# A circular 7x7 convolution of a 224x224 image on one core: reordered first loads, two weight jobs moved ahead of the first products, and a different place for one plane operation

## The chip, the cores and the metric

The kernel runs on one core of a Trainium2 chip. The metric is the device time of one execution in microseconds; lower is better. The core has a matrix engine (PE in the profile, with its weight loads shown as PEld), a vector engine (DVE), an activation engine (ACT), a general engine (POOL) and a queue engine (SP) that here mostly issues transfers between HBM and on-chip memory. The matrix engine writes into PSUM, an on-chip memory of eight banks; DVE and ACT move its results out ("evacuate" them), and each bank can be written again only once its evacuation is done.

## The reference

The input x is one image of 224 x 224 pixels with 96 channels, and w is a 7 x 7 kernel of 96 x 96 weights, both in bf16. The reference multiplies their two-dimensional Fourier transforms and transforms back, so the result is a circular convolution: the rows and columns before the first are the last ones.

```python
wp = jnp.pad(w, ((0, H - K), (0, W - K), (0, 0), (0, 0)))
Xf = rfft2(x.astype(f32), axes=(1, 2))
Wf = rfft2(wp.astype(f32), axes=(0, 1))
Yf = jnp.einsum('bhwi,hwio->bhwo', Xf, Wf)
y = irfft2(Yf, s=(H, W), axes=(1, 2)).astype(bf16)
```

## The kernel before

The kernel transforms along the image's rows only (h), in eight blocks of 28 rows with an overlap of six, and does the taps along w as shifted products with a minimal-filter scheme. A block's transform has 17 frequencies (`NS`), numbered s; frequency 0 and 16 are real (`REAL`) and cost fewer operations, the others are complex and use three products instead of four. The width is cut into seven tiles of 32 columns (`NT`), numbered t.

One tile goes through these steps. Its pixels are loaded by two transfers for each half of the blocks (`load_x`: 112 rows and 6 rows of 3,072 values each). The PE multiplies them with a Fourier matrix `Fm`, which a dozen small operations build at the start, and DVE or ACT evacuate the result into `xf` (functions `a_bank` and `f_jobs`). For groups of up to three frequencies (`JGB`), function `jit` makes three DVE operations, the "plane operations": the first and second write sums and differences of `xf` into the tile `J`, and the third adds parts of `J` into its planes 5 and 6. For every frequency, `b_round` then issues the products of `J` and `xf` with the transformed weights `WF` into two banks, an ACT copy with a factor (tile `tt_`), two DVE combinations `u` and `v`, and a sum of `u` and `v` into `yf`, which POOL does, or DVE in those rounds of tiles 2 to 6 that have plane operations (`ydve`). `yf` is written to a scratch array in HBM, read back as `tt` in another layout, multiplied with the inverse matrix `Gm`, evacuated into `yo` and stored (`c_jobs`).

The transformed weights are made by `prep_jobs(gi)` for six groups of frequencies (`PGRP`). The weights are loaded first, in five column pieces of two transfers each (`wdma`). A job of `prep_jobs` is four small PE products of the raw weights `wq` with a matrix `Em`, and one evacuation into `WF`; every group has 12 such jobs, and all but the first then have one DVE subtraction `WF<-WF` for each complex frequency. `evac` chooses DVE or ACT for an evacuation by running sums of costs, `load["v"]` and `load["a"]`.

All instructions of an engine run in the order in which the program issues them (`_Ordered`). At the start SP issues the wrap-around columns (`xh_bufs`, six columns left of the first tile, two transfers for each half), then the first half of the first tile's pixels, then the weights, then the second half. Every transfer of SP takes the next of eight completion counters in turn, so the ninth transfer is issued only when the first has landed, the tenth when the second has, and so on. The PE runs 17 products of zeros (`warm`), the wrap-around products, those of the first pixel half, 22 more products of zeros, the 48 products of weight group 0, those of the second half, and then the rounds. Tiles 0 and 1 run together, four rounds apart (`LAG`): from round 4 on, a round of tile 0 and one of tile 1 alternate. Within a round, `mid` and `end` run waiting jobs from lists with due times (`add`, `pace`): weight jobs of the next group and pixel jobs of tiles 1 and 2. For tiles 0 and 1 the plane operations of a group are put behind a round's `v` (`bursts`): two of the three in one round, and the third in the next round (`rest`), for both tiles alike. In a round with two plane operations the POOL sum waits for the second (line 580).

The steps that the change touches are lines 178 to 181 (first loads), 577 to 580 (what the POOL sum waits for), 707 to 711 (zero products and the jobs before the first products), 744 and 745 (due times of the weight jobs) and 795 to 797 (how many plane operations go into a round).

Of the kernel before, what the change touches and what calls it, by code (L numbers as in the profile page):

```python
# [56 lines left out]
def kernel(  # L57
# [117 lines left out]
    def load_x(t, jg):  # L175
        return load_rows(xbuf(t, jg), jg, t * 2 * TW, 2 * TW)

    wsrc = w.rearrange("kh kw i o -> (kh kw) (i o)")
    for jg in range(2):
        load_rows(xh_bufs[jg], jg, W - PAD, PAD)  # L180
    load_x(0, 0)
    wcut = [WC * c // NWC // 128 * 128 for c in range(NWC)] + [WC]
    wdma = []
    for c0, c1 in zip(wcut, wcut[1:]):
# [281 lines left out]
    def jit(t, g):  # L466
        s0, s1 = JGB[g]
        n = s1 - s0
        xf = xf_tiles[t][0:C]
        xv = xf.rearrange("c p r s w j -> c p r s (w j)")  # L470
        b = jcount[0] % 3 if t < 2 else (jcount[0] - 2 * len(JGB)) % 2
        jcount[0] += 1
        Jb = J_bufs[b][0:C].rearrange("c (k s q) -> c k s q", k=7, s=3)
        for s in range(s0, s1):
            jbuf[(t, s)] = Jb[:, :, s - s0]

        def sub(o, a, b, op, cost):
            def f():
                load["v"] += 170 + cost / 1.92
                return VE.tensor_tensor(out=o, in0=a, in1=b, op=op)  # L480
            return f
        x0, x1 = xv[:, 0, :, s0:s1], xv[:, 1, :, s0:s1]
        c0, c1 = max(s0, REAL[0] + 1), min(s1, REAL[1])
        i0, i1 = c0 - s0, c1 - s0
        pd, rd, sd, qd = x1.ap
        dpl = bass.AP(x1.tensor, x1.offset - NJ, [pd, [NJ, 2], rd, sd, qd])
        return [
            sub(Jb[:, 0:4, 0:n].rearrange("c (k r) s q -> c k r s q", r=2), dpl,
                x0.unsqueeze(1).to_broadcast([C, 2, 2, n, PP]), ALU.subtract, 4 * PP * n),
            sub(Jb[:, 4, i0:i1], xv[:, 0, 0, c0:c1], xv[:, 0, 1, c0:c1], ALU.add, PP * (c1 - c0)),  # L490
            sub(Jb[:, 5:7, i0:i1], Jb[:, 0:4:2, i0:i1], Jb[:, 1:4:2, i0:i1], ALU.add, 2 * PP * (c1 - c0)),
        ]
# [3 lines left out]
    def b_round(t, s, mid, end, ydve=False, planes=()):  # L496
# [26 lines left out]
        if s in REAL:  # L523
            for part in range(2):
                conv(b0, part * C, 0, part)
            SE.copy(out=tt_[:, 0:2 * C], in_=b0[:, 0:2 * C])
            mid()
            for mi, m in enumerate((2, 1)):
                for part in range(2):
                    conv(b1, (mi * 2 + part) * C, m, part)  # L530
            VE.tensor_tensor(out=yv.rearrange("p r m o -> p m r o"),
                             in0=tt_[:, 0:2 * C].rearrange("p (r o) -> p r o", o=C).unsqueeze(1).to_broadcast([128, 2, 2, C]),
                             in1=b1[:, 0:4 * C].rearrange("p (m r o) -> p m r o", m=2, r=2), op=ALU.add)
            load["a"] += 110 + 0.9 * 192
            load["v"] += 540
            for f in planes:
                f()
            end()
        else:
            v = tv_pool.tile([128, 2, 2, C], F32, name="v")  # L540
            if merge:
                conv(b0, 2 * C, 0, 0, both=True)
                conv(b0, 2 * C, 2, 0, add=True)
                conv(b0, 3 * C, 1, 0, add=True)
                conv(b0, 0, 0, 1)
                conv(b0, C, 0, 2)
                SE.mul(out=tt_[:], in_=b0[:, 0:4 * C], mul=-0.5)
                u, pr = tt_[:, 2 * C:4 * C].rearrange("p (m o) -> p m o", m=2), tt_[:, 0:2 * C]
            else:
                for part in range(3):  # L550
                    conv(b0, part * C, 0, part)
                conv(b0, 3 * C, 2, 0)
                conv(b0, 4 * C, 1, 0)
                u = tv_pool.tile([128, 2, C], F32, name="u")
                SE.mul(out=tt_[:, 0:3 * C], in_=b0[:, 0:3 * C], mul=-0.5)
                pr = tt_[:, C:3 * C]
            if puts:
                puts.pop(0)()
            if not merge:
                VE.scalar_tensor_tensor(out=u[:], in0=b0[:, 3 * C:5 * C].rearrange("p (m o) -> p m o", m=2), scalar=-0.5,  # L560
                                        in1=tt_[:, 0:C].unsqueeze(1).to_broadcast([128, 2, C]), op0=ALU.mult, op1=ALU.add)
            mid()
            for mi, m in enumerate((2, 1)):
                for pi, part in enumerate((1, 2)):
                    conv(b1, (mi * 2 + pi) * C, m, part)
            VE.scalar_tensor_tensor(out=v.rearrange("p m r o -> p m (r o)"),
                                    in0=pr.unsqueeze(1).to_broadcast([128, 2, 2 * C]), scalar=-2.0,
                                    in1=b1[:, 0:4 * C].rearrange("p (m q) -> p m q", m=2), op0=ALU.mult, op1=ALU.add)
            def ysum(eng):
                return eng.tensor_tensor(out=yv.rearrange("p r m o -> p m r o"), in0=v[:],  # L570
                                         in1=u.unsqueeze(2).to_broadcast([128, 2, 2, C]), op=ALU.add)
            if ydve:
                ysum(VE)
            last = None
            for f in planes:
                last = f()
            if not ydve:
                y = ysum(GE)
                if len(planes) > 1:
                    tc.add_manual_dep(y.ins, last.ins.name, SYNC, reason="sum after planes")  # L580
            load["a"] += 490 if merge else 410
            load["v"] += (560 if ydve else 250 if t < 2 else 0) + (560 if merge else 900)
            end()
# [120 lines left out]
    for p in range(3):  # L704
        for f in fj[p][0]:
            f()
    for n in (11, 11):
        warm(n)
    for f in prep_jobs(0):
        f()  # L710
    last = [f() for f in fj[0][1]]
    for jg in range(2):
        for d in load_x(1, jg):
            tc.add_manual_dep(d.ins, last[0].ins.name, SYNC, reason="second tile's pixels later")
# [26 lines left out]
    def add(a, b, jobs):  # L741
        qs.append([a, b, jobs, len(jobs)])

    for gi in range(1, len(PGRP)):
        add(2 * PGRP[gi - 1][0], 2 * PGRP[gi - 1][1] - (2 if gi == 1 else 1), prep_jobs(gi))
    for t in range(2):
        scr_tiles[t] = dr_pool.tile([TW, NJ, NS, 4 * C], BF16, name="scr")
    bursts = {}
# [9 lines left out]
    for r in range(NS + LAG):  # L758
        if r == 0:
            add(1, 5, fj[1][1])  # L760
            add(5, 9, fj[2][1])
        for p in range(3):
            if r == (1, 3, 5)[p]:
                new_xf(1, SH2[p], SH2[p + 1])
                fj = f_jobs(1, p)
                if p == 2:
                    for jg in range(2):
                        fj[jg][-1] = then_load(fj[jg][-1], 2, jg)
                add(2 * r + 1, 2 * r + (5, 5, 4)[p], fj[0] + fj[1])
        for p in range(3):  # L770
            if r == SH2[p + 1] + 1 - (p == 2):
                new_xf(2, SH2[p], SH2[p + 1])
                fj = f_jobs(2, p)
                if p == 2:
                    for jg in range(2):
                        fj[jg][-1] = then_load(fj[jg][-1], 3, jg)
                add(2 * r, 2 * r + (8, 7, 5)[p], fj[0] + fj[1])
        if r == PGRP[-2][1] + 1:
            assert not any(q[2] for q in qs[:len(PGRP) - 1])
            wtmp_cm.__exit__(None, None, None)  # L780
            t_pool = ctx.enter_context(tc.tile_pool(name="tt", bufs=NTT, side="right"))
            t2_pool = ctx.enter_context(tc.tile_pool(name="tt2", bufs=1, side="right"))
            yo_pool = ctx.enter_context(tc.tile_pool(name="yo", bufs=2, side="right"))
            g_pool = ctx.enter_context(tc.tile_pool(name="gp", bufs=1, side="right"))
            GA = g_pool.tile([KA, 4 * B], BF16, name="GA")
            GB = g_pool.tile([128, 2, 4 * B], BF16, name="GB")
            GE.memset(GA[:], 0.0)
            GE.memset(GB[:], 0.0)
        if r == NS + 3:
            queue_c(0)  # L790
        for t in range(2):
            s = r - LAG * t
            if not 0 <= s < NS:
                continue
            now = bursts.pop((r, t), ())
            now = jit(*now) if now else []
            now, rest = rest + now[:2], now[2:]
            both = LAG <= r < NS
            b_round(t, s, fills(qs, 2 * r + (t if both else 0)), fills(qs, 2 * r + (t if both else 1)), False, now)
    assert not rest and not bursts and nburst == 2 * len(JGB)  # L800
# [111 lines left out]
```

## Time and profile before

| what | value |
|---|---|
| median of three runs | 270.54 us (270.21 to 270.58) |
| the profiled execution's own time | 270.74 us |
| its span, first to last instruction | 269.0 us |
| granted PE clock, mean | 0.997 |
| PE busy | 257.9 us, 96% of the span, 5144 products |
| PE weight loads busy | 237.1 us, 88% |
| DVE busy | 214.3 us, 80% |
| ACT busy | 195.5 us, 73% |
| POOL busy | 99.4 us, 37% |
| HBM traffic | 24.65 MB read, 21.33 MB written |

The busy times of the engines overlap. PE's share is near the whole span, so the time is set by the PE's work and by the places where it waits; those are read from the chain of work that ended last and from the list of waits. The times in the views count from the first instruction of the core, and the whole execution takes 1.74 us more than the span.

### The profile page before, as it was taken

The page shows a single profiled execution, that of the slowest core. Times are in us where ns is not written, and L with a number is a line of the kernel's source. Part 1 is how long each engine was busy: PE and PEld are TensorE (multiplying, and loading weights), DVE is VectorE, ACT ScalarE, POOL GpSimd, SP SyncE. Part 2 cuts the span into 40 slices and gives each one's busy share as a digit, 9 for nine tenths or more (in the row PEclk, how much of TensorE's full clock was granted, in tenths as well). Part 3 has the DMA queues.
Part 4 walks back from the last instruction along what each step waited for, and adds up shares of the span by engine and source line. Part 5 has one row for each costly group of instructions (what it writes and reads, how often), then busy time and mean ns, then how long its engine had stood idle before and what let it go on. Part 6 is the DMA issues. An engine that isn't in the chain of part 4 may idle for free.

```text
span 269.0 us, 12171 instructions
## 1 busy us (share of the span) xinstructions
PE 257.9 (96%) x5144; PEld 237.1 (88%) x5144; DVE 214.3 (80%) x457; ACT 195.5 (73%) x483; POOL 99.4 (37%) x156
## 2 busy tenths in 40 slices
PE   8899999999999999999999999999998999899993
PEld 3679999999998999999999998989997989779862
DVE  5649998889899788778787888777887889778724
ACT  5549988587974578988988789886986864467113
POOL 7782315363647435322322222234132242522100
PEclk9999999999999999999999999999999999999998
DMA  6948011811111597987976486989658834888866
GB/s 171 230 129 217 6 46 46 243 47 67 46 46 50 163 276 135 294 249 206 289 207 198 133 246 192 250 223 332 224 151 152 255 98 154 198 231 212 223 118 205
DMA packets 47014, 46.78 MB, mean 174 GB/s; under 512 B 35286, under 2 KB 37986, under 8 KB 46960
## 3 DMA queue, kind: packets, MB, share of 16 engines
q1 hardware_dynamic: 44672, 43.94, 59.2%
q10 hardware_dynamic: 2288, 2.06, 2.8%
q8 instruction: 40, 0.66, 1.1%
q14 instruction: 14, 0.11, 0.1%
HBM read 24.65 MB, written 21.33 MB: 171 GB/s over the span
## 4 chain that ended last, share of the span: by engine, by line
PE 64%; DMA 12%; DVE 11%; ACT 7%; issue 3%; SPq 2%; DVEq 0%; ACTq 0%
PE pb L89 64%; DMA tt<-scr 5%; DMA wq<-in_w_dram 5%; DVE J L89 4%; ACT WF L89 3%; ACT xf L89 2%; DVE v L89 2%; DVE WF L89 2%; SPq L89 2%; DMA xf<-scrb 2%; DVE u L89 1%; DMA scrb<-yf 1%; DVE yf L89 1%; DVE xf L89 0%; DVE tt L89 0%
## 5 line engine op out<-in xcount | busy, mean ns | idle before, releaser
L89 PE MATMUL pb<-WF,J 96*128 96x96 bf16 x2821 | 162.6, 206 | 1.1 <-DVE J L89 0.9
L89 PEld LDWEIGHTS <-J 96*128 96x128 bf16 x2821 | 138.0, 98 | 10.5 <-issue 2.2
L89 POOL TENSOR_TENSOR yf<-v,u 128x384 bf16<-128x384 f32 x79 | 81.4, 1042 | 147.3 <-issue 86.9
L89 ACT CAST xf<-pb 96x408 bf16<-96x408 f32 (+3 forms) x145 | 67.8, 490 | 8.9 <-PE pb L89 5.3
L89 PE MATMUL pb<-WF,xf 96*128 96x96 bf16 x952 | 59.9, 206 | 0.5 <-ACT xf L89 0.5
L89 DVE TENSOR_TENSOR J<-xf 96x1824 bf16<-96x1824 bf16 (+1 forms) x84 | 56.9, 716 | 0.1
L89 PEld LDWEIGHTS <-xf 96*128 96x128 bf16 x952 | 47.0, 98 | 0.7 <-ACT xf L89 0.6
L89 PE MATMUL pb<-Fm,xn 118*128 118x136 bf16 (+3 forms) x640 | 45.5, 199 | 0.2 <-DVE u L89 0.2
L89 PE MATMUL pb<-tt,Gm 102*84 102x384 bf16 (+1 forms) x132 | 32.7, 327 | 2.4 <-DMA tt<-scr 2.3
L89 ACT CAST WF<-pb 96x480 bf16<-96x480 f32 (+1 forms) x59 | 29.1, 577 | 5.3 <-PE pb L89 5.3
L89 PEld LDWEIGHTS <-xn 118*128 118x128 bf16 x640 | 30.3, 97 | 0.3 <-issue 0.3
L89 ACT CAST J<-pb 84x384 bf16<-84x384 f32 (+1 forms) x64 | 27.6, 488 | 2.3 <-PE pb L89 2.0
L89 ACT CAST yo<-pb 84x384 bf16<-84x384 f32 (+1 forms) x63 | 26.9, 482 | 2.7 <-PE pb L89 2.7
L89 DVE TENSOR_TENSOR J<-J 96x912 bf16<-96x912 bf16 (+2 forms) x42 | 24.2, 576 | 0.0
L89 PE MATMUL pb<-wq 98*128 98x120 bf16 (+1 forms) x288 | 21.3, 226 | 0.3 <-DMA wq<-in_w_dram 0.3
L89 PEld LDWEIGHTS <-wq 98*128 98x128 bf16 x288 | 19.5, 151 | 0.8 <-issue 0.8
L89 PE MATMUL pb<-wu 128*128 128x512 bf16 (+1 forms) x75 | 16.5, 382 | 1.1 <-DVE ct L89 1.1
L89 PEld LDWEIGHTS <-wu 128*128 128x128 bf16 (+1 forms) x75 | 8.8, 119 | 7.7 <-issue 2.4
L89 DVE TENSOR_TENSOR yf<-v,u 128x384 bf16<-128x384 f32 x26 | 14.9, 571 | 0.9
L89 PEld LDWEIGHTS <-Gm 102*84 102x84 bf16 (+1 forms) x132 | 11.0, 117 | 3.5 <-DMA tt<-scr 2.9
L89 ACT COPY xf<-xf 96x816 bf16<-96x816 bf16 (+3 forms) x20 | 11.3, 632 | 0.0
L89 DVE CAST WF<-pb 96x480 bf16<-96x480 f32 (+1 forms) x13 | 7.5, 611 | 4.7 <-PE pb L89 4.7
(386 smaller groups left out, 234.4 us busy)
## 6 DMA issues: line engine op xcount, KB each, us to landing
scr<-yf SPq DMA_DIRECT2D x30, 288.0 KB
xn<-in_x_dram SPq DMA_DIRECT2D x12, 672.0 KB
tt<-scr SPq DMA_DIRECT2D x24, 336.0 KB
out_dram<-yo SPq DMA_DIRECT2D x12, 252.0 KB
out_dram<-J SPq DMA_DIRECT2D x12, 252.0 KB
tt<-scr SPq DMA_DIRECT2D x6, 288.0 KB
WF<-in_x_dram SPq DMA_DIRECT2D x2, 672.0 KB
out_dram<-tt SPq DMA_DIRECT2D x8, 168.0 KB
```

Source lines behind the costliest of these rows:

```text
L89: r = fn(*a, **k)
```

## The change

SP issues the first pixel half before the wrap-around columns instead of behind them. The second run of zero products has 20 products instead of 22. Two of the twelve jobs of weight group 1 are issued right behind the second pixel half's products and ahead of the first round, and both their evacuations are forced onto ACT (`load["v"] += 1e6`; the sums are set anew a few lines below); ten jobs and the three subtractions stay in the list. A tile-0 group's plane operations stay as they were (two in one round, the third in the next); a tile-1 group's, and those of tile 2's first group, are all three issued in one round. The POOL sum of a round now waits for the last plane operation in it even if there is only one.

```diff
@@ first loads @@
     wsrc = w.rearrange("kh kw i o -> (kh kw) (i o)")
+    load_x(0, 0)
     for jg in range(2):
         load_rows(xh_bufs[jg], jg, W - PAD, PAD)
-    load_x(0, 0)
@@ b_round @@
                 y = ysum(GE)
-                if len(planes) > 1:
+                if last is not None:
                     tc.add_manual_dep(y.ins, last.ins.name, SYNC, reason="sum after planes")
@@ before the rounds @@
-    for n in (11, 11):
+    for n in (10, 10):
         warm(n)
     for f in prep_jobs(0):
         f()
     last = [f() for f in fj[0][1]]
+    early = prep_jobs(1)
+    load["v"] += 1e6
+    for _ in range(2):
+        early.pop(0)()
...
     for gi in range(1, len(PGRP)):
-        add(2 * PGRP[gi - 1][0], 2 * PGRP[gi - 1][1] - (2 if gi == 1 else 1), prep_jobs(gi))
+        add(2 * PGRP[gi - 1][0], 2 * PGRP[gi - 1][1] - (2 if gi == 1 else 1), prep_jobs(gi) if gi > 1 else early)
@@ rounds of tiles 0 and 1 @@
             now = bursts.pop((r, t), ())
+            split = 2 if now and now[0] == 0 else 3
             now = jit(*now) if now else []
-            now, rest = rest + now[:2], now[2:]
+            now, rest = rest + now[:split], now[split:]
```

`now[0]` is the tile whose planes are made. In the order of instructions this gives: PE loses two zero products and has eight weight products moved ahead of the first round; ACT has two weight evacuations before the first round and one weight evacuation more than before by round 1, and DVE one fewer; further on, seven third plane operations stand ahead of the `u` and `v` that they followed, one pixel evacuation at round 3 goes from DVE to ACT and one at round 4 from ACT to DVE, and in later tiles a few evacuations change between DVE and ACT. POOL's order is the same.

## The prediction

> **What bounds the kernel now.** I read the page's busy shares first (PE 96%, none other above 88%), then the chain that ended last in order of time, the timelines around each place where it leaves the PE, and last the list of waits. The chain, up to the stretch in which the PE works alone:
>
> ```profile
> 3.40 6.14 DMA wq<-in_w_dram
> 9.55 6.52 DMA wq<-in_w_dram
> 16.07 0.14 issue
> 16.21 0.69 PE pb L89 x8
> ...
> 19.68 1.03 ACT xf L89 x2
> 20.71 0.05 issue
> 20.76 0.53 PE pb L89 x8
> 21.28 0.02 issue
> 21.31 0.32 ACT tt__556 L89
> 21.63 4.19 ACT WF L89 x9
> ...
> 43.28 0.28 DVE u L89
> 43.56 0.04 issue
> 43.60 6.79 PE pb L89 x171
> ...
> 57.47 0.91 DVE J L89
> 58.37 0.05 issue
> 58.42 17.60 PE pb L89 x395
> ...
> 86.48 0.90 DVE J L89
> 87.39 0.05 issue
> 87.43 89.21 PE pb L89 x1845
> ```
>
> The reader is to see three stretches. Up to 16.07 us the weights' transfers set the time. From 16.9 to 43.6 the chain runs through ACT's and DVE's evacuations without a pause: these set the time, the PE only just behind. From there the PE sets it, but for waits on a plane operation of DVE at 58.42, 82.54 and 87.43. Those are the PE's waits on J in the list of waits between 20 and 90 us, and the stretches say how full each engine is:
>
> ```profile
> PEld L89 <- DVE J L89: 1.4, 3, 0.6
> PEld L89 <- ACT xf L89: 0.6, 1, 0.6
> ```
>
> ```profile
> 1.75:4.00 2.25, 2.25 (x6) 0.76 (x5) 1.91 (x10) 2.24 (x3) 1.91 (x8) 1.00 0.81 173
> 4.00:6.00 2.00, 2.00 (x9) 0.89 (x8) 1.14 (x7) 0.48 (x2) 1.43 (x8) 1.00 0.91 289
> 6.00:13.25 7.25, 6.51 (x122) 4.62 (x121) 4.53 (x8) 3.62 (x8) 5.67 (x30) 1.00 1.04 233
> 20.75:46.00 25.25, 25.03 (x609) 24.92 (x610) 24.18 (x45) 22.98 (x57) 7.29 (x8) 1.00 0.26 72
> ```
>
> The columns are PE, PEld, DVE, ACT and POOL busy, granted clock, the transfer engines' share and GB/s. The transfer engines are full from 4 to 13 us; DVE, ACT and PE are all nearly full from 20.75 to 46.
>
> **First loads.** No transfer is added; SP issues the same sixteen in another order. Before 4.0 us the 16 transfer engines lose time: by the packets in the trace they did 23.6 engine-us from 1.8 to 4.0, of 35.2, so 11.6/16 = 0.72 us each, in gaps between the small wrap-around transfers (236 packets of 1152 bytes, mean 73 ns, 17.3 engine-us). Behind the pixels these packets would queue up without gaps. That bounds the gain from above at 0.72 us. Against it: the ninth transfer waits for the first to land. Now that is a small one (landed at 2.9 us); it becomes the 672 KB pixels, which landed 5.1 us after issue here and 4.9 us for the second tile's (20.24 to 25.18), so at 0.80 + 5.0 = 5.8. The tenth, the second large weight piece, waits for the six rows, 5.0 to 5.4 us after 1.24, so 6.3 to 6.6, instead of 4.62; its packets follow some 0.9 us later, at 7.2 to 7.5. The first piece (98 packets of 254 ns, 1.56 us on 16 engines) would be done at 7.0 to 7.3. So up to 0.5 us may be lost to an empty queue, and from below the whole step at -0.4 us if every landing comes late. I take **0.3 us** of gain, between the ends and nearer the packets' row. The wrap-around pixels land later (about 6.1 for 4.0); the PE's zero products cover that to 6.5 and the POOL fill that releases the PE at 7.64 covers a further 1.1 us. If that cover went, each 0.1 us would be 0.1 us of PE.
>
> **Zero products.** Two less take 2 x 0.213 = 0.43 us from the PE's run, whose last ends at 15.72 and then waits 0.49 us for the weights. They cost or gain nothing by themselves; they let the PE start as early as 15.3. The gap stays under 1 us and the row of granted clock shows 1.00 on both sides of such gaps, so I expect no lower clock.
>
> **Two jobs ahead of the first products.** Eight products at 62 ns, 0.5 us, fill the gap 20.30 to 20.76 in which the PE waits for ACT's xf. But ACT decides here. Before: xf ends at 20.70, idle 0.19, the Gm activation, 0.04 idle, the tt copy, nine casts at a spacing of 0.46 to 25.82. After: two casts, activation, copy, eight casts: one cast more (0.46) less 0.23 idle, so **0.2 us later** at the end of the casts. DVE has a cast less, but its subtraction at 25.85 starts 0.03 us after ACT's last cast, and from there DVE has no idle until 33.33, where it waits 0.44 for ACT's tt. The PE's lead of 0.5 us is then eaten: its smallest margins against these evacuations are 0.36 at 30.3, 0.05 at 32.2 and 0.05 at 35.9. Bounds: 0.5 gained if the chain does not bind, 0.46 lost if no idle is filled.
>
> **Third operation of tile-1 groups.** Seven are moved ahead of the next `u` and `v`. Two matter. At round 3 the third (40.68, 0.46 us) leaves the stretch that ends in `u` at 43.55, for which the PE waits 0.38 at 43.60; a pixel cast of 0.48 that DVE loses makes room earlier. Up to 0.38 is gained. POOL's sum, now behind the third, moves 0.4 us into the subtraction at 38.15, which already takes 1.01 against 0.65 where no POOL sum stands beside it. I take **0.2 us** gained, ends 0.38 and -0.1. At 87.43 the PE waits 0.53 for the third that began at 86.40. Issued behind the second (85.75) and with POOL waiting for it, it takes 0.62 as at 31.51, not 0.97, and ends at 86.3, before the PE's 86.9. The whole wait goes: **0.5 us**, ends 0 and 0.53; next late is the `u` at 86.02, half a microsecond later, against a bank margin of over 1.9. The waits at 58.42 (0.65) and 82.54 (0.24) belong to tile-0 groups and stay.
>
> ```profile
> 86.40 0.97 DVE L89 TENSOR_TENSOR J<-J 96x912 bf16<-96x912 bf16 x1
> ...
> 87.43 0.33 PEld L89 LDWEIGHTS <-J 96*128 96x128 bf16 x7 [0.51 <-DVE J L89]
> ```
>
> **The POOL sums.** In seven rounds the sum starts about 0.5 us later, and behind it the next round's sum, whose reader is the `scr` transfer, not urgent. At 77.43 it would lie longer beside three subtractions (0.84 for the first now, some 1.0 then), and from there DVE has no idle to the wait at 82.54: **0.1 us** lost, ends 0 and 0.32. In rounds with one plane operation the sum would start at 58.5 instead of 57.83, where it ran 1.40 us beside the third; its end moves 0.2, against a `u` that waits for ACT anyway: nothing.
>
> [...] The trace: a third operation begun while a POOL sum runs took 0.97 to 0.99 us, alone 0.62, less than the overlap would cost if it stood still. [...]
>
> **Sum.** -0.3 + 0.2 - 0.2 - 0.5 + 0.1 = **-0.7 us**. The profiled execution of 270.74 (span 269.0 and 1.74 around it) would become 270.04; it stands 0.20 above the median of 270.54, so I predict **269.8**. Later evacuations that change engine lie where PE margins are above 0.9 us; I take them at nothing, with 0.2 to either side.
>
> **Rivals.** (1) The weights land when they did: the chain's 16.07 stays, the last piece being issued when the eighth transfer lands. For it speaks that the engines are full from 4 us; against it the 0.72 us. Sum -0.4: 270.1. (2) The empty queue costs more than the gaps gave: slower. Place: the issue of the tenth transfer. If the pixels land 6.5 us after issue instead of 5.0, its packets come at 1.24 + 6.5 + 0.9 = 8.6, 1.5 us after the first piece is done at 7.1; less 0.4 for the gaps that are filled, the weights land 1.1 later. With the other terms (-0.4) that is +0.7: 271.2. It decides once the weights land after 17.0 (0.54 + 0.4 behind 16.07). For it speaks that the landings hang on the slowest of 16 engines (6.38 to 7.46 for the pixels now); against it that both measured landings are near 5 us. (3) DVE and POOL stand still for each other: the subtraction at 38.15 loses 0.4 more, the group behind it as much as it gained, the ones at 77.43 0.3 instead of 0.1. Sum -0.3 + 0.2 + 0.2 - 0.5 + 0.3 = -0.1: 270.4. The 0.97 for an overlap of 0.48 us speaks half for it.
>
> **Numbers.** My own case 0.56, (1) 0.15, (2) 0.16, (3) 0.13. 0.2% is 0.54 us, about what a measurement of this kernel can tell from no change: faster is below 270.0, slower above 271.1. My case lies at 269.2 to 270.1, (1) and (3) within 0.2%, (2) above it in its greater part. Faster 0.57, same 0.26, slower 0.17. The range takes in (1) and (3), the full gains of the terms (-0.72 - 0.1 - 0.38 - 0.53 = -1.7) nearly, and the lower half of (2): 268.9 to 271.1.
>
> **What would show it.** Right: weight products start at 15.8 to 16.0, not 16.21; no PE wait ahead of the first xf products; ACT's casts of group 1 end 0.2 us later relative to the start of the weight products; no wait at 87.4 and the third there near 0.62 us; waits of about 0.65 and 0.3 us at the tile-0 groups. Wrong: the start at 16.2 or later, new waits of the PE between 24 and 43 us, or a third of a tile-1 group still on the chain.

## The result

The changed kernel took 271.96 us (median of 22 runs, 270.37 to 274.08), the kernel before 270.56 us beside it (22 runs, 269.22 to 273.52). The ratio is 1.0063, with a 95% interval of 1.0044 to 1.0081: slower by 0.6%, 1.7 us (the medians lie 1.40 us apart). The forecast was 269.8 us, within 268.9 to 271.1, and faster. The profiled execution took 271.87 us (span 270.2, granted clock 0.997), so it stands for the median. The ratios, here and in the table below, leave out seven runs counted as slow, three of them of first_third (273.8 to 274.5 us), and are not the ratios of the medians.

The chain that ended last, of the changed kernel, as far as the lines shown of before went:

```profile
1.25 4.80 DMA WF<-in_x_dram
...
7.18 4.26 DMA wq<-in_w_dram
11.52 5.16 DMA WF<-in_x_dram
16.75 0.68 PE pb L89 x8
17.45 0.50 ACT WF L89
17.97 2.26 ACT WF L89 x5
20.22 1.02 ACT xf L89 x2
21.25 0.91 ACT WF L89 x2
22.63 3.69 ACT WF L89 x8
...
42.20 1.38 issue
43.58 0.38 DVE J L89
44.28 7.04 PE pb L89 x175
...
58.34 0.91 DVE J L89
59.30 17.61 PE pb L89 x395
...
82.86 0.66 DVE J L89
83.57 8.45 PE pb L89 x224
```

The weights' products start at 16.75 us, not 16.21. The chain names the second pixels (issued at 11.52) ahead of them, but these landed only at 18.15 us; what landed just before the products was the last packet of the weights, at 16.61. The PE's release near 44 us comes 0.68 later than before, the one near 59 us 0.88 later and the one near 83 us 1.03 later, so more is lost on the way. Only at 87.4 us did what was promised happen. DVE and then the PE's weight loads there:

```profile
86.92 0.62 DVE L89 TENSOR_TENSOR J<-J 96x912 bf16<-96x912 bf16 x1
```

```profile
87.55 0.40 PEld L89 LDWEIGHTS <-xf 96*128 96x128 bf16 x8
87.89 0.35 PEld L89 LDWEIGHTS <-J 96*128 96x128 bf16 x7
```

The third operation takes 0.62 us instead of 0.97, and the load behind it waits for nothing. Two stretches of the changed kernel (columns as in the prediction), and the PE's longest waits between 20 and 90 us:

```profile
1.75:4.00 2.25, 2.25 (x6) 0.76 (x5) 1.91 (x10) 2.24 (x3) 1.91 (x8) 1.00 0.95 281
20.75:46.00 25.25, 24.32 (x591) 23.93 (x589) 23.85 (x44) 23.56 (x60) 5.10 (x7) 1.00 0.26 73
```

```profile
PEld L89 <- DVE J L89: 0.9, 2, 0.6
PEld L89 <- issue: 0.6, 1, 0.6
PEld L89 <- DMA xn<-in_x_dram: 0.5, 1, 0.5
```

The transfer engines are busier early on (0.95 against 0.81), as the first step meant. But between 20.75 and 46 us the PE is busy for 24.32 us, not 25.03. The wait for xf is gone from the list; waits for a transfer of pixels and for what the profile calls issue have come. The pixels are the second tile's: fifteen of the sixteen engines had landed them by 25.94 us and the last at 27.24, where before all had by 25.18. Such a late landing comes without the change too: in bias2908, the kernel before but for one number of the balance, the last engine landed them at 26.81 us and the PE waited 0.4 us. Measured from the start of the weights' products, the product that starts at 181.28 us in before and at 181.87 us here stands 0.05 us apart (165.07 and 165.12 us). So of the 1.2 us between the two spans 0.54 lie ahead of the weights' products, and the rest lies behind 182 us.

### The profile page after: what moved, and what is told of

Its sections match the earlier page's. It is cut to its first block, busy times and chain, and to the rows that moved or that the text cites. A ratio compares the mean times of both kernels' runs of the same rounds, so it can differ in the third digit from the quotient of the medians.

```text
span 270.2 us, 12160 instructions
## 1 busy us (share of the span) xinstructions
PE 258.1 (96%) x5142; PEld 237.2 (88%) x5142; DVE 214.4 (79%) x457; ACT 195.5 (72%) x483; POOL 96.2 (36%) x156
## 4 chain that ended last, share of the span: by engine, by line
PE 58%; DVE 15%; DMA 13%; ACT 7%; issue 4%; SPq 1%; POOL 0%; DVEq 0%; ACTq 0%
PE pb L89 58%; DMA tt<-scr 5%; DVE J L89 5%; DMA WF<-in_x_dram 4%; ACT WF L89 3%; DVE WF L89 3%; DVE v L89 3%; ACT xf L89 2%; DVE u L89 2%; DVE yf L89 2%; DMA wq<-in_w_dram 2%; DMA xf<-scrb 2%; SPq L89 1%; DMA scrb<-yf 1%; POOL yf L89 0%
## 5 line engine op out<-in xcount | busy, mean ns | idle before, releaser
L89 POOL TENSOR_TENSOR yf<-v,u 128x384 bf16<-128x384 f32 x79 | 78.9, 1010 | 150.3 <-issue 86.5
L89 DVE TENSOR_TENSOR J<-xf 96x1824 bf16<-96x1824 bf16 (+1 forms) x84 | 57.6, 725 | 0.1
L89 ACT CAST WF<-pb 96x480 bf16<-96x480 f32 (+1 forms) x60 | 29.7, 579 | 5.9 <-PE pb L89 5.9
L89 DVE CAST WF<-pb 96x400 bf16<-96x400 f32 (+1 forms) x12 | 6.9, 607 | 5.3 <-PE pb L89 5.3
```

The lines of the kernel that those rows point to most:

```text
L89: r = fn(*a, **k)
```

## The experiments

Eighteen kernels were run, in five groups; each group shared its runs of the kernel before. Seven theories were set against each other. About the first step: A, the second pixels, issued earlier, hold up the weights' tail; E, the order of the loads moves nothing on the mean; F, a longer gap of the PE ahead of the weights' products lowers the granted clock in some executions; G, the order of the loads costs in itself. About the early jobs: B, the stretch from 20 to 44 us loses; C, the loss is in the dealing of late evacuations to DVE and ACT. About the third operation: D, what one group gains the others give back.

| kernel | parts of the change in it | runs | median us | ratio to before, 95% interval |
|---|---|---|---|---|
| first_only | first loads, 10 and 10 zero products | 12 | 270.57 | 1.0018 [0.9991, 1.0045] |
| early_only | early jobs | 12 | 271.15 | 1.0039 [1.0013, 1.0064] |
| third_only | third operation, all groups | 12 | 270.23 | 1.0008 [0.9984, 1.0032] |
| after_hold3 | all; second pixels a piece later | 6 | 272.54 | 1.0086 [1.0056, 1.0117] |
| early_comp | early jobs, counted in the balance | 12 | 270.47 | 0.9991 [0.9964, 1.0017] |
| bias2908 | none; the early jobs' late dealing | 12 | 271.57 | 1.0021 [0.9988, 1.0054] |
| first_third | all but the early jobs | 12 | 270.99 | 1.0005 [0.9972, 1.0037] |
| third_last | third operation, round 16 only | 12 | 270.32 | 0.9996 [0.9966, 1.0026] |
| after_again | all | 12 | 271.66 | 1.0062 [1.0031, 1.0094] |
| after_comp | all, early jobs counted | 12 | 271.02 | 1.0018 [0.9992, 1.0044] |
| third_15 | third operation, round 15 only | 12 | 269.79 | 0.9975 [0.9959, 0.9991] |
| early_comp_third15 | early jobs counted, round 15 only | 12 | 269.44 | 0.9963 [0.9942, 0.9984] |
| best_first | the row above and first loads | 12 | 270.38 | 1.0013 [0.9988, 1.0039] |
| best_third_all | early jobs counted, all groups | 12 | 270.39 | 1.0007 [0.9986, 1.0029] |
| third_old_sum | third operation, sum's wait as before | 12 | 270.11 | 0.9990 [0.9971, 1.0010] |
| best_old_deal | early jobs not counted, round 15 | 12 | 270.43 | 1.0000 [0.9978, 1.0023] |
| best_zero10 | early_comp_third15, 10 and 10 | 12 | 269.86 | 0.9997 [0.9973, 1.0021] |
| best_order11 | early_comp_third15, pixels first | 12 | 270.28 | 1.0010 [0.9982, 1.0038] |

### The parts alone

Each is the kernel before with one part of the change's diff: first_only has the moved `load_x(0, 0)` and `(10, 10)`; early_only the `early` lines and the `add` that takes them; third_only the `split` lines and `last is not None`.

> The kernel before with one part of the change alone: first pixels ahead of the wrap-around ones, 10 and 10 zero products. Theory A (the start is late because the second pixels, whose issue hangs on the third large weight piece, are now issued 1.4 us earlier, at 11.5 us, and share the transfer engines with the tail of the weights): the weights' last landing is 16.6 us, the weight products start at 16.7 to 16.8 instead of 16.2, and the time is 0.4 to 0.7 us above before. Theory B (the start is not the cause; the two early jobs are): the start may still be at 16.75, but the lead of the later stretches absorbs it, and the time is within 0.3 us of before.

> The kernel before with the two jobs of the second weight group ahead of the first products, nothing else. Theory A: weights land at 16.07 as before; the evacuations of the second group end 0.2 us later, the time is 0 to 0.4 us above before. Theory B (the early jobs bring the stretch from 20 to 44 us out of step: a PE wait of some 0.6 us at 26.7 and a larger one at 44): 0.6 to 1.2 us above before, with that wait of 0.5 us or more between 24 and 30 us.

> The kernel before with the third plane operation of the tile-1 groups moved, nothing else. Both theories: no PE wait at 87.4 us (0.53 before); 0.4 to 0.8 us below before. If it is not below before, the gain of the wait that goes is given back by the later sums on POOL, and a new wait is to be seen between 90 and 255 us.

The early jobs alone cost 0.39%, the first loads 0.18% with zero in the interval, and the third operation gains nothing. The PE's trace of early_only has no wait of 0.6 us at 26.7, so theory B as written fell: the gap ahead of the first xf products shrinks from 0.63 to 0.13 us, three waits of 0.16 to 0.23 us between 29 and 32 us take that back, and the release near 43 us stands as in before, measured from the start of the weights' products (27.33 us behind it, 27.39 in before). What it has in addition is a wait of 0.23 us at 190.7, in a place that the change's lines do not touch, and longer waits behind 195 us. In third_only the wait at 87.4 is gone (0.53), but those near 43 and 82.5 us grew from 0.38 to 0.68 and from 0.24 to 0.39, and one of 0.21 us at 39 us is new.

### The second pixels held back

```diff
-HOLD = 2
+HOLD = 3
```

> The changed kernel with the second pixels waiting for the fourth large weight piece instead of the third. Theory A: their issue moves from 11.5 to about 13.0 us, the last weight piece lands at 14.9 to 15.6 us instead of 16.6, the weight products start 0.9 to 1.4 us earlier, and the time falls by 0.8 to 1.5 us against the changed kernel, below before. Theory B: the weights land earlier too, but the stretch behind them keeps its waits; under 0.5 us gained.

The landings came out as theory A had them: the second pixels were issued at 13.64 instead of 11.52 us and the last weight piece landed at 15.06 instead of 16.61. The time did not follow: it is no better than the changed kernel's. The list of waits between 18 and 20 us of this kernel says why:

```profile
PEld L89 <- DMA WF<-in_x_dram: 0.6, 1, 0.6
```

The second pixels now land at 18.76 (18.15 in the changed kernel), and the PE, done with the weights early, waits for them. In this trace, then, one of two transfers goes last, and which of them does not matter much.

### The dealing of late evacuations

`evac` gives each evacuation to the engine whose sum of costs would be lower. Ahead of the rounds the sums are set to 3000 and 0. Two jobs issued ahead of that line are no longer counted: in before one of the first jobs went to DVE (660) and one more to ACT (568), so from there on DVE's sum stands 92 lower against ACT's than it did. A list of all 364 decisions shows two neighbours near 30 us exchanged and then nothing until eleven close calls near the end of the list, which the traces place between 182.4 and 216 us (the expectations below say 187). early_comp counts the two jobs, bias2908 takes 92 off in the kernel before:

```diff
@@ early_comp, on early_only @@
-    load["v"], load["a"] = BIAS, 0.0
+    load["v"], load["a"] = BIAS + 660, 568.0
@@ bias2908, on before @@
-    load["v"], load["a"] = BIAS, 0.0
+    load["v"], load["a"] = BIAS - 92, 0.0
```

> The two early jobs alone, as in the run that had them alone, but the balance that deals evacuations to DVE and ACT starts at 3660 and 568 instead of 3000 and 0, as if it had counted the two jobs. From the fortieth evacuation on, each goes to the engine it had in the kernel before; of the eleven between about 187 and 217 us that the early jobs had moved from one engine to the other none is moved now. Theory C (the loss is that dealing): within 0.3 us of before, and the PE's idle time behind 195 us back from 6.9 to about 6.0 to 6.5 us. Theory B (the loss is in the stretch from 20 to 44 us, ACT's extra cast): 0.5 us or more above before, as the early jobs alone.

> The kernel before with nothing but the start of the balance between DVE and ACT moved from 3000 to 2908, which deals eleven evacuations between about 187 and 217 us (and two neighbours near 30 us) as the early jobs do; the jobs themselves stay where they were. Theory C: 0.4 to 0.8 us above before, with the PE's wait of 0.2 us near 190.7 us that the kernels with early jobs show. Theory B: within 0.2 us of before.

With the jobs counted, the early jobs cost nothing (0.9991 against 1.0039); with the dealing alone and no early jobs, the interval of bias2908 reaches from -0.1% to +0.5%, and its trace has the wait at 190.6. The same change was then made in the whole changed kernel, beside a second measurement of it, and undone in the best kernel:

> The changed kernel itself, unchanged, for the comparison with the next one beside it: 1.2 to 1.8 us above before, as in its first measurement.

> The changed kernel with the start of the balance at 3660 and 568, as if it had counted the two early jobs; the eleven evacuations behind 187 us go to the engines that they have in the kernel before. Theory C (the dealing behind 187 us is the loss): 0.8 to 1.5 us below the changed kernel, within 0.4 us of before. Theory B (the loss is in the stretch up to 84 us: the late start, and waits that grew at 26.7, 44 and 59 us): under 0.4 us below the changed kernel, still 0.8 us or more above before.

> The kernel with early jobs and the third operation moved in round 15 alone, with the balance started at 3000 and 0 as in the changed kernel, so that the eleven evacuations behind 187 us change engine. Theory C: 0.4 to 0.9 us above the kernel with the balance that counts the jobs (0.9963), so 0.998 to 1.000 of before. Rival (the dealing costs only together with the other losses): 0.996 to 0.997.

Counting the jobs takes 0.44% off the changed kernel (1.0062 to 1.0018), 1.2 us and so within what theory C asked for, though what is left stands 0.5 us above before, a little more than its 0.4; not counting them costs the best kernel 0.37% (0.9963 to 1.0000, measured in two groups). All three pairs point one way. How it comes about can be read where the first of the eleven lies. DVE in best_old_deal, then the PE there:

```profile
182.86 0.43 DVE L89 CAST xf<-pb 96x272 bf16<-96x272 f32 x1
183.21 0.54 DVE L89 CAST yo<-pb 84x384 bf16<-84x384 f32 x1
...
189.72 0.34 DVE L89 SCALAR_TENSOR_TENSOR u<-pb,tt__5700 128x192 f32<-128x192 f32 x1
```

```profile
189.55 0.50 PE L89 MATMUL pb<-WF,xf 96*128 96x96 bf16 x8
190.11 0.34 PE L89 MATMUL pb<-Fm,xn 118*128 118x136 bf16 x3
```

And the same two views of early_comp_third15, in which that pixel evacuation is ACT's:

```profile
182.83 0.54 DVE L89 CAST yo<-pb 84x384 bf16<-84x384 f32 x1
...
189.33 0.34 DVE L89 SCALAR_TENSOR_TENSOR u<-pb,tt__5700 128x192 f32<-128x192 f32 x1
```

```profile
189.51 0.50 PE L89 MATMUL pb<-WF,xf 96*128 96x96 bf16 x8
189.85 0.34 PE L89 MATMUL pb<-Fm,xn 118*128 118x136 bf16 x3
```

A cast of 0.43 us came onto DVE ahead of a group of plane operations. From there DVE is 0.39 us late without a pause up to the `u` at 189.72, and the PE's next product waits for a bank. That explains 0.2 us. The rest lies behind 195 us, where the stores and loads of `scr`, `scra` and `scrb` set the PE's waits. Summed over the PE's products behind 195 us, the time by which a product starts later than the one before it would let it (one column in 1/2.4 ns, the slope between the starts of products in before, which follow 42.5 ns apart for 96 columns, 162.9 for 384 and 215.8 for 512) is 8.22 us on the mean of the six traces with the changed dealing (7.69 to 8.43) and 7.30 us on that of thirteen with the dealing of before (6.42 to 8.10; without first_third, whose clock was halved there). The largest piece lies behind 258 us, around the last `scrb` load, 1.2 against 0.7 us. The first product of that load in best_old_deal, and in early_comp_third15, where it follows without a wait:

```profile
260.23 0.99 PE L89 MATMUL pb<-xf,GB 128*112 128x384 bf16 x5 [0.57 <-DMA xf<-scrb]
```

```profile
258.62 0.99 PE L89 MATMUL pb<-xf,GB 128*112 128x384 bf16 x5
```

Which of the eleven evacuations makes that wait longer was not tried.

### The third operation, group by group

```diff
@@ third_last, on before; third_15 has NS - 2 for NS - 1 @@
-            now, rest = rest + now[:2], now[2:]
+            now, rest = rest + now[:3 if r == NS - 1 else 2], now[3 if r == NS - 1 else 2:]
@@ third_old_sum, on third_only @@
-                if last is not None:
+                if len(planes) > 1:
```

> The kernel before with the third operation moved in the last group of tile 1 alone, the one at 87.4 us. Theory D (moving the third in every group of tile 1 gains the wait of 0.53 us at 87.4 and gives it back in waits at 39.0, 43.5 and 82.8 us, which grew by 0.2, 0.3 and 0.15): the wait at 87.4 goes, those three stay as before, and the time is 0.3 to 0.6 us below before. Rival: the PE's gain at 87.4 is lost behind, in the waits on transfers after 195 us, and the time is within 0.2 us of before.

That run named the wrong group: its trace still has the wait of 0.53 at 86.7 us. The operation that the PE waits for there is that of round 15's group.

> The kernel before with the third operation moved in one group alone, that of round 15, which is the one that the PE waits for at 87.4 us (the run before this moved round 16's, and the wait stayed). Theory D: the wait of 0.53 us goes, 39, 43.5 and 82.8 us stay as they were, 0.3 to 0.6 us below before. Rival: the gain is lost in the waits on transfers behind 195 us: within 0.2 us of before.

0.9975, with an interval that ends below 1: the wait is gone, the others are as they were, and the gain of 0.25% is a little over the 0.53 us of the wait (0.20%). Then all groups instead of one, in a kernel that differs in nothing else:

> The kernel before with the two early jobs, the balance that counts them, and the third operation moved in round 15's group alone; the first loads as before. If both gains hold (0.4 of the PE's wait at 20.3 us, 0.5 at 87.4, less 0.4 in the stretch from 24 to 44 us): 0.4 to 0.9 us below before. If what is gained ahead of 195 us is lost in the transfers behind it: within 0.2 us of before.

> The same kernel (early jobs, balance that counts them, old first loads), but the third operation moved in all groups of tile 1 as the change does. Theory D: the waits at 39, 43 and 82.5 us grow by 0.2, 0.3 and 0.15 us, and the time is 0.4 to 0.9 us above the kernel that moves round 15 alone, that is 0.998 to 1.000 of before. Rival: the other groups give nothing back, 0.996.

> The kernel before with the third operation moved in all groups of tile 1, but POOL's sum waiting only where it waited before, so not for a round's single plane operation. If the growth of the waits at 43 and 82.5 us comes from the sums that now wait for a tile-0 group's late third operation, the waits at 58 and 82.5 us go back to 0.65 and 0.24 us; if it comes from the move on DVE itself, they stay at 0.68 near 43 and 0.39 near 82.5 us. Time: 0.997 to 1.001 of before.

early_comp_third15 beats both kernels of the case, with 269.44 us. Moving the operation in all groups takes the gain away (1.0007, in another group). The wait that the change adds to the POOL sum of a round with one plane operation is not the reason: without it the PE's waits are 0.71 near 43 us and 0.39 near 82.5 us, as in third_only. In a round that has all three operations the sum waits for the last of them in third_old_sum as well, so that run does not undo the sum's move behind the third. The reason stands in the timelines of DVE and POOL around 38 us, here of before:

```profile
38.15 2.15 DVE L89 TENSOR_TENSOR WF<-WF 96x960 bf16<-96x960 bf16 x3
```

```profile
37.64 1.00 POOL L89 TENSOR_TENSOR yf<-v,u 128x384 bf16<-128x384 f32 x1 [4.62 <-DVE J L89]
```

and here of third_only:

```profile
37.82 2.54 DVE L89 TENSOR_TENSOR WF<-WF 96x960 bf16<-96x960 bf16 x3
...
41.21 1.96 DVE L89 TENSOR_TENSOR J<-xf 96x1824 bf16<-96x1824 bf16 x2
43.09 0.34 DVE L89 SCALAR_TENSOR_TENSOR u<-pb,tt__1161 128x192 f32<-128x192 f32 x1
```

```profile
37.70 1.00 POOL L89 TENSOR_TENSOR yf<-v,u 128x384 bf16<-128x384 f32 x1 [4.76 <-DVE J L89]
```

In before the sum (37.64 to 38.64) overlaps the three subtractions for 0.49 us, and in third_only (37.70 to 38.70) for 0.88 us. The sum now waits for the third operation, which has taken the place of a pixel cast that went to ACT: measured from the start of the weights' products it starts 0.42 us later (21.85 for 21.43), and the subtractions start where they did (21.97 and 21.94). The subtractions take 0.39 us longer: exactly the added overlap. The next group's first operations take 1.96 instead of 1.75 us, beside 0.69 instead of 0.48 us of the sum at 40.9. So the third operation leaves the stretch behind the subtractions (0.46), and what it frees and a little more is spent where operations of DVE run beside POOL's sums (0.39 and 0.21 us more). At 77.5 us it is the same, two subtractions in 1.56 instead of 1.41 us, and the wait at 82.5 us grows by the same 0.15.

### The first step in the best kernel

best_first adds both halves of the step to early_comp_third15; the other two add one half each, `(10, 10)` or the moved `load_x(0, 0)`. first_third is the changed kernel without the early jobs.

> The changed kernel without the early jobs: first pixels first, and the third plane operation moved. If the parts add up, 0 to 0.5 us above before (the two alone gave +0.2 and -0.1 with half widths of 0.7). If early jobs are the whole of the loss, no difference from before within 0.3 us. If the parts work on each other (a late start with an early group), over 0.7 us above.

> The kernel with early jobs, balance that counts them and the third operation moved in round 15 alone (0.9963 of before), and in addition the first pixels first and 10 and 10 zero products. Theory E (the order of the first loads moves neither the weights' nor the second pixels' last landing on the mean; over the runs so far the products start at 16.07 us with the old order and 16.17 with the new): within 0.3 us of 0.9963 of before. Rival (the second pixels, issued earlier, delay the weights): 0.4 us or more above that.

> The kernel with early jobs, balance that counts them and the third operation moved in round 15 alone (0.9963 of before), old order of the first loads, but 10 and 10 zero products instead of 11 and 11. Theory F (the longer gap on the PE ahead of the weights' products brings a lower granted clock in some executions): 0.999 to 1.002 of before, and 3 or more of 12 runs with a mean clock under 0.9955. Theory G (the order of the loads costs): 0.996 to 0.997, at most 2 such runs.

> The same kernel with the first pixels ahead of the wrap-around ones, and 11 and 11 zero products as before. Theory F: 0.996 to 0.997 of before, at most 2 runs of 12 with a mean clock under 0.9955. Theory G: 0.999 to 1.002.

first_third lies where the sum of its parts lies, with a wide interval. In the best kernel the step costs half a per cent (0.9963 to 1.0013, in two groups), and each half alone a good part of it, with intervals that overlap both those rows. The zero products alone met theory F's range of time and the order alone theory G's, and both had two runs with a mean clock under 0.9955. So neither theory F nor G is shown; E fell, as far as it said that the step costs nothing. The traces say only this: over the eleven with the old order and 11 and 11 zero products the last weight packet landed at 15.65 us on the mean (14.91 to 16.76), over the seven with the new order at 15.86 (15.30 to 16.61), and the second pixels at 18.19 and 18.13. Nothing lands earlier that anything waits for.

## Why the prediction was wrong

If the parts add, the fourteen kernels that are made of whole parts give each part's cost (least squares over their ratios, weighted by the intervals; the residuals are as small as the intervals allow, a weighted sum of squares of 6.7 with 9 left over). Since kernels of a group share their runs of before, the half widths are rough.

| step | predicted us | measured us |
|---|---|---|
| first loads and zero products | -0.3 | +0.6 ± 0.4 |
| two jobs ahead | +0.2 | 0.0 ± 0.4 |
| late evacuations that change engine | 0 ± 0.2 | +0.9 ± 0.4 |
| third operation of all tile-1 groups, with the POOL sums | -0.6 | +0.1 ± 0.4 |
| (round 15's group alone) | -0.5 | -0.7 ± 0.3 |
| sum of the first four | -0.7 | +1.6 |

**Late evacuations.** The step that failed most is one sentence: "Later evacuations that change engine lie where PE margins are above 0.9 us; I take them at nothing". The margin of the evacuation itself was the wrong thing to look at. A cast of 0.43 us that moves onto DVE delays everything queued behind it on DVE, here for 7 us, down to a `u` that had no margin. Nor is there any margin to read behind 195 us, where transfers that start later end later: the last `scrb` load, for which the PE then waits, starts at 256.30 us in before and at 257.58 in the changed kernel, and ends at 260.35 and 261.65.

**First loads.** The gaps did close, but the loss set against that came with it, and larger than taken. The second large piece was issued at 6.07 us, and the transfer engines stood half idle from 6.5 to 8.0 us; before and then the changed kernel:

```profile
6.50:8.00 1.50, 0.80 (x12) 0.62 (x11) 0.41 (x2) 0.49 (x1) 1.23 (x12) 1.00 1.02 227
```

```profile
6.50:8.00 1.50, 1.41 (x15) 0.87 (x14) 0.41 (x2) 0.50 (x1) 1.24 (x12) 1.00 0.55 108
```

It is so in every trace: a share of 0.46 to 0.68 in the eight with the new order, 0.98 to 1.09 in the twelve with the old one. Packets that had ended by 6.5 us came to 1.16 to 1.21 MB with the new order and 0.96 to 1.07 MB with the old one, by 8.0 us to 1.35 to 1.37 and 1.33 to 1.48 MB: the lead was gone. So the term that failed is the net gain of 0.3 us, taken between up to 0.72 gained and up to 0.5 lost: by the shares of these two traces some 0.6 us of all sixteen engines were gained up to 6.5 us (0.95 for 0.81 of 2.25 us, 1.02 for 0.91 of the next 2.5) and 0.7 lost behind it (0.55 for 1.02 of 1.5 us). Large pieces 1 to 4 did land earlier, by 0.5 to 1.0 us on the mean of the same traces and by 1.3 to 1.6 us in the profiled execution (9.90 for 11.19, 12.98 for 14.55), but the fifth, which ends the weights, did not. The second pixels are released by the third large piece, so they were issued 1.40 us earlier (11.52 for 12.92), and the last packet of piece 5, on one engine, landed at 16.61, after all others of that piece had landed by 14.91. Holding the pixels back only moves the wait to them. The second error was to take 16.07, one execution's landing, for a fixed time, and 0.3 us for a gain that can be seen in it: over the traces that landing lies anywhere from 14.9 to 16.8, and in half of those with 11 and 11 zero products these, not the weights, end last (products at 15.7). Rival (2), slower through an empty queue at the tenth transfer, named the right place and the right sign, but not the size: its condition, pixels that land 6.5 us after issue, did not come (4.8 in the profiled execution), and the weights landed 0.2 us later on the mean, not 1.1.

**Zero products.** The two products less are 0.43 us, as taken, though at 0.216 us from start to start in before, not 0.213. "Cost or gain nothing by themselves", and a gap under 1 us: in the profiled execution it was 1.46 us, and on the mean 0.78 us over the six traces with the step, 0.21 over the eleven with the old order and 11 and 11. The granted clock there stayed at 1.00 in these traces. Whether the two products less are part of the +0.6 is open.

**Two jobs ahead.** The mechanism was right: no wait ahead of the xf products, and the PE's lead eaten between 24 and 32 us. ACT's last cast of group 1 ended 9.61 us behind the start of the weights' products in before and 9.57 behind it in the changed kernel, so not 0.2 later but the same; the idle time of ACT that was filled made up for the whole cast.

**Third operation and sums.** At 87.4 us the whole wait went, as worked out (third_15's third operation ends at 85.96, 0.34 us being the earlier start: 86.3 on before's clock, as forecast). At round 3 the sign was wrong: -0.2 foreseen, a wait 0.3 us longer in fact. The term that failed is the one taken beside it, the sum's move into the subtraction: it was counted as going partly, and the overlap was paid in full, 0.39 us there and 0.21 more in the next group's first operations. The third operation of 0.97 us, from which a part was read, had met two sums; only the one already running counted, with 0.48 us left, and it cost 0.35. At 82.54 the 0.1 was 0.15. For this step rival (3) was the right one, with its 0.4 at 38.15. The subtractions' 0.39 us more for 0.39 us more overlap agrees with it, and so does what is told of all traces below. The waits at 58.4 and 82.5 us stayed, at 0.60 and 0.38 for the forecast 0.65 and 0.3.

## What to carry to other kernels

Where a planner keeps running sums to deal work to engines, work moved across the point where the sums are reset changes choices far away: list the decisions of both kernels, and put the sums right before measuring the move itself. A move that helps at one wait should be made at that wait alone; done everywhere it changed what runs beside what, and lost the gain. Landings of transfers are to be taken from several executions: a gain smaller than their spread, on a chain where another transfer ends 2 us later anyway, is no gain.

## What the hardware showed that was not expected

**DVE beside a POOL sum.** Three kinds of DVE operation were followed through all twenty traces: subtractions of 96x960 (0.64 us alone), first plane operations of 96x1824 (1.10) and third ones of 96x912 (0.62). One that begins while a POOL sum runs takes longer by what is left of the sum, less 0.12 to 0.14 us; so it is for all 228 of them with more than 0.13 us left, from 0.14 to 0.90 us (in before a subtraction with 0.50 us left took 1.01 us). One that began before the sum loses nothing (38 third operations, at most 0.01 us), and then the sum takes longer, by what is left of the DVE operation less 0.13 us (1.35 for 1.00 us with 0.46 left, at 31.67 us in before). So in these traces the one that begins second paid the whole overlap, but for that 0.13 us.

**A halved clock behind a wait.** In one of the twenty traces, that of first_third (mean clock 0.99, span 271.9 us), the PE waited for a `scr` load, and its clock was half for 3.4 us afterwards. The wait, and the stretches behind it (columns: PE busy, clock, transfer engines' share, GB/s):

```profile
204.52 0.56 PE L89 MATMUL pb<-tt,Gm 102*84 102x384 bf16 x2 [1.56 <-DMA tt<-scr]
```

```profile
204.00:206.00 2.00, 1.48 (x16) 0.72 0.79 100
206.00:207.00 1.00, 1.00 (x15) 0.50 0.35 70
207.00:208.00 1.00, 1.00 (x16) 0.50 0.95 240
208.00:209.00 1.00, 1.00 (x17) 0.86 1.15 275
```

A longer wait, in bias2908, left the clock at 1.00:

```profile
232.65 0.52 PE L89 MATMUL pb<-tt,Gm 102*84 102x384 bf16 x2 [1.85 <-DVE J L89]
```

So the length of the wait alone does not decide it. Where it lies may. In the other nineteen traces the full clock lasts 259.4, 262.8 or 266.2 us from its first rise (262.83 in before and in the changed kernel): lengths that lie 3.4 us apart and are 76, 77 and 78 times 3.41 us. In first_third it lasts 58 such steps, then the half clock one, then the full clock 18. There the step that ended as the clock fell, at 204.87 us, held the whole wait and 1.84 us without a product in all; in bias2908 the wait fell across two steps, the fuller of which held 1.53 us. Of all steps up to 255 us that were followed by the full clock none held more than 1.68 us, but one near the end of best_old_deal held 1.91, so no limit can be read from them, and what made the clock fall is not shown.

**How often.** A mean granted clock under 0.9955 goes with a long time (in the first comparison the nine such runs of the changed kernel average 273.2 us, its other thirteen 271.4). Runs with both halves of the first step had it 33 times in 88, with one half 4 times in 24, and all others, before included, 23 times in 277. That is a part of the step's +0.6 us: with the runs under 0.9955 left out on both sides (and the first comparison, whose runs of before have no clock on record) the fit of the parts gives +0.3 ± 0.2 us for the first step, and still +0.7 ± 0.3 for the late evacuations and -0.6 ± 0.3 for round 15's group; its residuals are larger than the intervals allow, so this is rough. Where in those executions the clock falls was not recorded, and why this step should bring it on is open. One candidate, not shown, is the gap ahead of the weights' products: the step of 3.41 us around it held 1.06 to 1.57 us without a product in six traces with both halves, and 0.75 to 1.18 us in the eleven with neither; against it, after_hold3, with 0.77 us there, had three such runs in six.
